# A two-layer MLP's output turned into rows by VectorE in 32x32 blocks instead of by TensorE

## The chip, the cores and the metric

The kernel runs on one core of a Trainium2 chip. The metric is the device time of one execution in microseconds. Before the change the median of three runs is 1579.02 us (1576.81 to 1579.77). Names of engines: PE is TensorE (PEld its weight loads), DVE is VectorE, ACT is ScalarE, POOL is GpSimd, SP is the engine that issues most DMAs. All arithmetic is fp32; a product that has to be exact enough is made of three single-pass products of parts (high x high, high x low, low x high).

## The reference

Attention through 32 packed queries per head, then two MLPs over 4608 tokens (8 batches of 576) of 512 channels, with 2048 hidden channels. The change touches the last MLP's output and its gate.

```python
p_packed = sm_attn(p, k, v)
out = sm_attn(q, p_packed, p_packed)                 # 8 batches, 8 heads, 576 tokens, 64
x = out.transpose(0, 2, 1, 3).reshape(B * S, H * D)  # 4608 x 512
h = x @ w_in                                         # first MLP, 512 -> 2048
g = h * (1.0 / (1.0 + np.exp(-h)))
x = g @ w_out                                        # 2048 -> 512
h = x @ w_in2                                        # second MLP
relu6 = np.clip(h + 3.0, 0.0, 6.0)
g = h * relu6 / 6.0
return (g @ w_out2).astype(np.float32)               # 4608 x 512
```

The weights arrive as 64-bit floats, and the kernel itself turns them into fp32 parts.

## The kernel before

Attention and the first MLP are woven into nine token blocks (`block`, L868): eight of 512 tokens, one for each batch, and a ninth of the 64 last tokens of all batches. A block holds its first layer's result as four accumulators in PSUM, [128 channels, 512 tokens] each. Tokens stand there in the order i, p for token 4p + i, because the queries were read that way. At the block's end the accumulators are copied to SBUF, two by ACT (L909) and two by DVE (L911), and stored to a scratch tensor `x1d` in DRAM (L912), channels first. A planner places the attention steps of the following blocks between the matmuls.

Meanwhile `Prep` (L244) prepares the second MLP's weights, 16 units for `w_in` and 16 for `w_out`, a step at a time: load (L264), two ACT operations, two on DVE, an addition on POOL that joins the two halves of each number into `c` (L293), sums on DVE (L296 to L299), the high parts on ACT, the low parts on POOL, three stores to DRAM.

The second MLP (`Second`) works on five pairs of token blocks, three of 2 x 512 tokens and two of 2 x 384. Both of its layers use a scheme of seven products for a 2 x 2 split of the weights and tokens. For each pair there are two passes:
- The hidden pass (`hidden`, L1034) has 16 chunks of seven products, six matmuls each (L1107 to L1109). Each chunk uses three PSUM banks of eight. ACT and DVE add the products up; then ACT makes relu(h + 3) (L1051) and, one product later, DVE makes min(., 6) x h (L1054).
- The projection (`project`, L1157) has seven products in four steps each, twelve matmuls a step (L1197 to L1200). An operand is split into a high part on ACT (L1145) and a low part on DVE (L1150) two steps before its use. The sums of the products are `o1`, `ou`, `ov` and `oc`, each [128 channels, 2, N tokens].

The output must be rows of tokens, but these sums have channels on the partitions. `store` (L1218) takes 128 tokens: four 128x128 transposes on TensorE against an identity into a PSUM bank (L1224), a copy on ACT that multiplies by 1/6 (L1226), a store from SP (L1230 for the eight batches, L1234 for the block of last tokens). `ou` and `ov` are stored in the last steps of their own projection (L1209), `oc` and `o1` during the next pair's hidden pass (L1114); in the last pair `oc` goes in the projection too and only `o1` is left for the end.

Weights stream into four tiles `ws` (L967 to L969); a tile is loaded again, from SP, as soon as TensorE has used it. Every engine's instructions run in the order in which this code writes them.

Of the kernel before, what the change touches and what calls it, by code (L numbers as in the profile page):

```python
# [18 lines left out]
def tile_pack_attention_two_mlps(ctx: ExitStack, tc, q, k, v, p, w_in1, w_out1, w_in2, w_out2, out):  # L19
# [8 lines left out]
    nc = tc.nc  # L28
# [41 lines left out]
    nc.vector.memset(mask, 0.0)  # L70
    for h in range(HQ):
        nc.vector.memset(mask[h * NP:(h + 1) * NP, h, :], 1.0)
    three = const.tile([P, 1], F32, name="three")
    nc.vector.memset(three, 3.0)
    d1s, d2s = {}, {}
    x1d = [dram.tile([KC, P, T], F32, name=f"x1d{j}", tag=f"x1d{j}") for j in range(NBLK)]

# [166 lines left out]
    class Prep:  # L244
# [11 lines left out]
        def load(self, u):  # L256

            kind, f, h = self.units[u]
            raw = self.pool.tile([P, 2 * T], I32, tag="praw", name="praw", bufs=2)
            for n, to in enumerate(raw.rearrange("p (n r) -> n p r", n=2)):  # L260
                src = self.src[kind](f + n * HF)
                if kind == "out":
                    src = src.rearrange("p a (r f) -> p (a r) f", r=4)
                nc.sync.dma_start(out=to.rearrange("p (r f) -> p r f", r=2), in_=src[:, h:4:2])  # L264
            raws["p", u] = raw

        def step(self):
# [6 lines left out]
        def all(self):  # L274
            self.load(0)
            for _ in range(6):
                yield
            for u, (kind, f, h) in enumerate(self.units):
                key = "p", u
                c = self.pool.tile([P, 8, P], F32, tag="c8", name="c8")  # L280
                hi = self.pool.tile([P, S7, P], F32, tag="hi7", name="hi7", bufs=2)
                conv_begin(key, self.room)
                yield
                yield
                conv_bits(key)
                yield
                if u + 1 < len(self.units):
                    self.load(u + 1)
                yield
                x, r = (t.rearrange("p (n r f) -> p n r f", n=2, r=2) for t in raws.pop(key))  # L290
                a = c[:, 0:4].bitcast(I32)
                a = a.rearrange("p (n r) f -> p n r f", n=2) if kind == "in" else a.rearrange("p (r n) f -> p n r f", n=2)
                nc.gpsimd.tensor_add(out=a, in0=x, in1=r)  # L293
                yield

                nc.vector.tensor_add(out=c[:, 4], in0=c[:, 2], in1=c[:, 3])  # L296
                nc.vector.tensor_sub(out=c[:, 6], in0=c[:, 0], in1=c[:, 2])
                nc.vector.tensor_sub(out=c[:, 5], in0=c[:, 4], in1=c[:, 0])
                nc.vector.tensor_sub(out=c[:, 7], in0=c[:, 1], in1=c[:, 5])  # L299
                yield  # L300
                nc.scalar.copy(out=hi[:, 0:2].bitcast(F32R), in_=c[:, 0:2])
                nc.scalar.copy(out=hi[:, 2:7].bitcast(F32R), in_=c[:, 3:8])
                yield
                nc.gpsimd.tensor_sub(out=c[:, 0:2].bitcast(F32R), in0=c[:, 0:2], in1=hi[:, 0:2])
                nc.gpsimd.tensor_sub(out=c[:, 3:8].bitcast(F32R), in0=c[:, 3:8], in1=hi[:, 2:7])
                yield
                yield
                to = w2[kind][f].rearrange("s p f -> p s f")
                nc.sync.dma_start(out=to[:, :, h * P:(h + 1) * P], in_=hi)
                nc.sync.dma_start(out=to[:, 0:2, (2 + h) * P:(3 + h) * P], in_=c[:, 0:2])  # L310
                nc.sync.dma_start(out=to[:, 2:7, (2 + h) * P:(3 + h) * P], in_=c[:, 3:8])
# [556 lines left out]
    def block(j, nxt, boundary):  # L868

        acc = [ps_acc.tile([P, T], F32, tag=f"acc{e}", name=f"acc{e}") for e in range(KC)]  # L870
        gs = {}
        fat = j in (0, B)
        total = ((6 if not fat else 12) + 12) * NF
        at_ = [0]

        def tick(n, calm=False):
            at_[0] += n
            plan.tick(n, at_[0] / total, calm)

        def projects(f, between=None):  # L880
            w = made["out", f] if j == 0 or f % 2 == 0 else have_out.pop((j, f))
            g = gs.pop(f)
            for e in range(KC):
                project(f, e, g, w, acc)
                tick(3)
                if e == 1 and between:
                    between()
            projected[0] = j * NF + f
        for f in range(NF):
            if not fat and f % GF == 0:  # L890
                plan.finish(lambda key: key[:3] == ("m", j, f // GF))
            g = hidden(j, f, lambda: tick(3), nxt)
            gs[f] = split_g(g)
            tick(0, True)
            nxt(f, True)
            if f == 2:
                left()
            if f >= 2:
                projects(f - 2, lambda: nxt(f, False))
            nxt(f, True)  # L900
        boundary()
        for f in (NF - 2, NF - 1):
            projects(f)
        plan.finish()
        for e2 in range(0, KC, 2):
            o = gp.tile([P, 2, T], F32, tag="x1", name="x1", bufs=2)
            for e in (e2, e2 + 1):
                if e % 2:
                    nc.scalar.copy(out=o[:, 1, :], in_=acc[e])  # L909
                else:  # L910
                    nc.vector.tensor_copy(out=o[:, 0, :], in_=acc[e])  # L911
            leave.append(lambda e2=e2, o=o: nc.sync.dma_start(out=x1d[j][e2:e2 + 2].rearrange("e p t -> p e t"), in_=o))  # L912
        if j == B:
            left()
# [23 lines left out]
    class Second:  # L938
# [95 lines left out]
        def hidden(self, n):  # L1034
# [13 lines left out]

            def act(f, part, h):
                r = self.left.tile([P, N], F32, tag="hr", name="hr", bufs=4)  # L1050
                nc.scalar.activation(out=r, in_=h, func=AF.Relu, bias=three)  # L1051

                def gate():
                    nc.vector.scalar_tensor_tensor(out=self.g[part, f // 2][:, f % 2], in0=r, scalar=6.0, in1=h, op0=ALU.min, op1=ALU.mult)  # L1054

                soon(1, gate)

# [34 lines left out]
            for i, (f, k) in enumerate(seq):  # L1092
# [18 lines left out]
                    self.load_w()  # L1111
                run_later()
                after(f, k)
                if i % S7 == 5 and self.out:  # L1114
                    self.out.pop(0)()
            while later:
                run_later()
            while self.out:
                self.out.pop(0)()


        def t1(self, fd):
# [34 lines left out]
        def project(self, n):  # L1157
            X, Y, Z = [], [], []
            N = NS[n]
            o1, ou, ov, oc = (self.left.tile([P, 2, N], F32, tag=tag, name=tag) for tag in ("o1", "ou", "ov", "oc"))  # L1160
            last_pair = n == NPAIR - 1
            early = [lambda t=t: self.store(ATS[n] + N + t * P, {0: ou, 1: ov}, t) for t in range(N // P)]
            if last_pair:
                early += [lambda t=t: self.store(ATS[n] + t * P, {0: oc}, t) for t in range(N // P)]

            def after(k):
                for i in range(2):
# [11 lines left out]
                        nc.scalar.copy(out=oc[:, i], in_=X[i])  # L1179
                    elif k == 4:  # L1180
                        nc.vector.tensor_add(out=o1[:, i], in0=o1[:, i], in1=Y[i])
                if k == 5:
                    nc.gpsimd.tensor_add(out=ov, in0=ov, in1=o1)

            for s in range(FD * S7):
                k, fd = ORDER_P[s // FD], s % FD
                w, ro = self.weights(), self.ro.pop(s)
# [18 lines left out]
                    self.split(s + RO - 1)  # L1206
                if self.prep and (s < 2 * FD or s // FD % 2 == 0):
                    next(self.prep, None)
                if s > FD * 5 and early:  # L1209
                    early.pop(0)()  # L1210
                yield
            if self.prep:
                for _ in self.prep:
                    pass
            for t in range(N // P):
                self.out.append(lambda t=t: self.store(ATS[n] + t * P, {1: o1} if last_pair else {0: oc, 1: o1}, t))

        def store(self, col, halves, t):  # L1218

            ps = self.bank()  # L1220
            lo, hi = min(halves) * 2 * P, (max(halves) + 1) * 2 * P
            for h, src in halves.items():
                for e in range(2):
                    nc.tensor.transpose(ps[:, (2 * h + e) * P:(2 * h + e + 1) * P], src[:, e, t * P:(t + 1) * P], ident)  # L1224
            o = self.left.tile([P, DM], F32, tag="st", name="st", bufs=3)
            nc.scalar.mul(out=o[:, lo:hi], in_=ps[:, lo:hi], mul=1.0 / 6.0)  # L1226
            j, c = divmod(col, T)
            if j < B:
                i = c // P
                nc.sync.dma_start(out=out[j * S:j * S + T, :].rearrange("(p i) e -> p i e", i=NI)[:, i, lo:hi], in_=o[:, lo:hi])  # L1230
            else:
                rows = out.rearrange("(b s) e -> b s e", s=S)[:, T:S, lo:hi]
                for i in range(P // TAIL):
                    nc.sync.dma_start(out=rows[c // TAIL + i], in_=o[i * TAIL:(i + 1) * TAIL, lo:hi])  # L1234

        def run(self):
            self.near = opened(ctx, "second_n", side="right", reuse_waits="tile")
# [7 lines left out]
            for n in range(NPAIR):  # L1245
# [2 lines left out]
                self.hidden(n)  # L1248
                for _ in self.projected:
                    pass  # L1250
            for fn in self.out:
                fn()


    class Feed:
# [262 lines left out]
```

## Time and profile before

| | before |
|---|---|
| median of three runs | 1579.02 us |
| the profiled execution's own time | 1579.41 us |
| its span, first to last instruction | 1577.6 us |
| PE busy, matmuls | 1531.3 us (97%) |
| DVE busy | 1018.2 us (65%) |
| ACT busy | 793.8 us (50%) |
| POOL busy | 191.1 us (12%) |
| mean granted clock of PE | 0.990 |

Busy time is the time in which an engine executes something. A matmul's own duration overlaps with the next one's, so what a matmul costs is read from the distance between starts. A releaser is the instruction that ended an engine's wait. The second MLP's first matmul starts at 862.58 us.

### The profile page before, as it was taken

The page shows a single profiled execution, that of the slowest core. Times are in us where ns is not written, and L with a number is a line of the kernel's source. Part 1 is how long each engine was busy: PE and PEld are TensorE (multiplying, and loading weights), DVE is VectorE, ACT ScalarE, POOL GpSimd, SP SyncE. Part 2 cuts the span into 40 slices and gives each one's busy share as a digit, 9 for nine tenths or more (in the row PEclk, how much of TensorE's full clock was granted, in tenths as well). Part 3 has the DMA queues.
Part 4 walks back from the last instruction along what each step waited for, and adds up shares of the span by engine and source line. Part 5 has one row for each costly group of instructions (what it writes and reads, how often), then busy time and mean ns, then how long its engine had stood idle before and what let it go on. Part 6 is the DMA issues. An engine that isn't in the chain of part 4 may idle for free.

```text
span 1577.6 us, 22053 instructions
## 1 busy us (share of the span) xinstructions
PE 1531.3 (97%) x7724; PEld 1246.2 (79%) x7724; DVE 1018.2 (65%) x1630; ACT 793.8 (50%) x1279; POOL 191.1 (12%) x171
## 2 busy tenths in 40 slices
PE   6899998999999999999999999999999999999998
PEld 3577766767777777778878888888888888999998
DVE  5876455755576465653452678767876687777775
ACT  4876545744566546654353334543454344444443
POOL 1433011111120111112232000000000000000000
PEclk9899999999999999999999999999999999999999
DMA  8899686977678776758596567666766676888886
GB/s 218 276 283 299 218 229 169 273 213 210 180 227 229 227 171 194 243 173 247 178 336 192 193 202 239 208 213 206 232 211 213 203 224 222 268 288 263 268 250 203
DMA packets 394639, 358.55 MB, mean 227 GB/s; under 512 B 155040, under 2 KB 281760, under 8 KB 394528
## 3 DMA queue, kind: packets, MB, share of 16 engines
q1 hardware_dynamic: 383152, 342.45, 72.2%
q10 hardware_dynamic: 11376, 14.68, 2.9%
q8 instruction: 62, 1.02, 0.3%
q14 instruction: 49, 0.40, 0.1%
HBM read 295.17 MB, written 61.87 MB: 226 GB/s over the span
## 4 chain that ended last, share of the span: by engine, by line
PE 86%; DMA 4%; ACT 4%; DVE 3%; issue 1%; SPq 1%; POOL 0%; DVEq 0%; POOLq 0%; ACTq 0%
PE acc L857 8%; PE b L1109 7%; PE b L1107 7%; PE b L1108 7%; PE b L1197 7%; PE acc L858 7%; PE acc L859 7%; PE b L1199 7%; PE b L1200 7%; PE hps L834 4%; PE hps L836 4%; PE hps L835 4%; PE abank L407 1%; PE abank L495 1%; PE b L1224 1%
## 5 line engine op out<-in xcount | busy, mean ns | idle before, releaser
L850 DVE TENSOR_TENSOR gl<-hps,gh 128x512 fp32r<-128x512 f32 x144 | 98.9, 687 | 170.0 <-ACT gh L849 169.6
L1199 PE MATMUL b<-ro,ws 128*128 128x512 f32 (+1 forms) x560 | 207.6, 371 | 0.0
L1107 PE MATMUL b<-xc,ws 128*128 128x512 f32 (+1 forms) x560 | 207.0, 370 | 0.0
L1200 PE MATMUL b<-ro,ws 128*128 128x512 f32 (+1 forms) x560 | 205.8, 367 | 0.0
L1109 PE MATMUL b<-xc,ws 128*128 128x512 f32 (+1 forms) x560 | 205.7, 367 | 0.0
L1108 PE MATMUL b<-xc,ws 128*128 128x512 f32 (+1 forms) x560 | 205.6, 367 | 0.0
L1150 DVE TENSOR_TENSOR ro<-g,ro 128x1024 fp32r<-128x1024 f32 (+1 forms) x140 | 161.6, 1160 | 48.4 <-ACT ro L1145 48.1
L1145 ACT CAST ro<-g 128x1024 fp32r<-128x1024 f32 (+1 forms) x140 | 133.2, 966 | 96.3 <-PE b L1197 45.4
L842 ACT ACTIVATE hps<-hps 128x512 f32<-128x512 f32 x144 | 84.0, 583 | 136.7 <-PE hps L836 133.2
L1197 PE MATMUL b<-ro,ws 128*128 128x512 f32 (+1 forms) x560 | 138.4, 368 | 0.5 <-DVE ro L1150 0.4
L857 PE MATMUL acc<-gh,wo 128*128 128x512 f32 x288 | 117.9, 409 | 0.9 <-ACT gh L849 0.9
L857 PE MATMUL acc<-gh,wr 128*128 128x512 f32 x288 | 118.2, 411 | 0.0
L1109 PEld LDWEIGHTS b<-xc,ws 128*128 128x128 f32 x560 | 105.1, 188 | 13.2
L1108 PEld LDWEIGHTS b<-xc,ws 128*128 128x128 f32 x560 | 105.2, 188 | 12.9
L1199 PEld LDWEIGHTS b<-ro,ws 128*128 128x128 f32 x560 | 105.2, 188 | 12.8
L1107 PEld LDWEIGHTS b<-xc,ws 128*128 128x128 f32 x560 | 105.1, 188 | 12.9
L1200 PEld LDWEIGHTS b<-ro,ws 128*128 128x128 f32 x560 | 105.2, 188 | 12.8
L1197 PEld LDWEIGHTS b<-ro,ws 128*128 128x128 f32 x560 | 102.4, 188 | 15.5 <-DVE ro L1150 2.4
L858 PE MATMUL acc<-gl,wo 128*128 128x512 f32 x288 | 113.6, 395 | 0.8 <-DVE gl L850 0.8
L858 PE MATMUL acc<-gl,wr 128*128 128x512 f32 x288 | 114.2, 397 | 0.0
L859 PE MATMUL acc<-gh,wr 128*128 128x512 f32 x288 | 113.9, 395 | 0.0
L859 PE MATMUL acc<-gh,wo 128*128 128x512 f32 x288 | 113.5, 394 | 0.0
(256 smaller groups left out, 2952.2 us busy)
## 6 DMA issues: line engine op xcount, KB each, us to landing
ws<-w2in SPq DMA_DIRECT2D x280, 256.0 KB, 3.2
ws<-w2out SPq DMA_DIRECT2D x280, 256.0 KB, 3.3
wi<-w1i SPq DMA_DIRECT2D x80, 512.0 KB, 5.5
wo<-w1o SPq DMA_DIRECT2D x64, 512.0 KB, 5.4
x1d<-x SPq DMA_DIRECT2D x18, 512.0 KB, 7.4
w1i<-win SPq DMA_DIRECT2D x16, 512.0 KB, 6.4
praw<-in_moe_w_in_dram SPq DMA_DIRECT2D x32, 256.0 KB, 5.6
praw<-in_moe_w_out_dram SPq DMA_DIRECT2D x32, 256.0 KB, 4.9
```

What stands on the lines that cost most here:

```text
L850: nc.vector.tensor_sub(out=gl, in0=g, in1=f32(gh))
L857: mm(acc[e], lhsT=w[:, 0, s], rhs=gh, start=first, stop=False)
L858: mm(acc[e], lhsT=w[:, 0, s], rhs=gl, start=False, stop=False)
L859: mm(acc[e], lhsT=w[:, 1, s], rhs=gh, start=False, stop=last)
L1107: mm(ps, lhsT=wh, rhs=xs[k][:, 0, c], start=first, stop=False, skip_group_check=True)
L1108: mm(ps, lhsT=wh, rhs=xs[k][:, 1, c], start=False, stop=False, skip_group_check=True)
L1109: mm(ps, lhsT=wl, rhs=xs[k][:, 0, c], start=False, stop=last, skip_group_check=True)
L1145: nc.scalar.copy(out=t[:, 0], in_=v)
L1150: nc.vector.tensor_sub(out=t[:, 1], in0=self.operand(s), in1=f32(t[:, 0]))
L1197: mm(acc[i], lhsT=wh, rhs=ro[:, 1, f], start=False, stop=last, skip_group_check=True)
L1199: mm(acc[i], lhsT=wh, rhs=ro[:, 0, f], start=first, stop=False, skip_group_check=True)
L1200: mm(acc[i], lhsT=wl, rhs=ro[:, 0, f], start=False, stop=False, skip_group_check=True)
```

## The change

The output is turned by VectorE. Its transpose works on 32x32 blocks: of a [128, N] source each block of 32 partitions and 32 columns is turned in place. So one partition group g of 32 channels gives, for each 32 tokens, 32 rows of 32 channels, on the partitions of that same group. For these to be neighbours in a row of the output, the columns of `w_out` are dealt anew when they are prepared: group g of every one of the four 128-channel parts belongs to the output columns from 128 g on. Four transposes (two for each of two sums) fill a tile `rows[t]` of [128, N/32, 128], and four stores, one for each g, each carry 32 partitions in pieces of 512 bytes.

- `Prep` loads `w_out` in runs of 64 numbers instead of 128, and POOL's addition writes runs of 32.
- The 1/6 goes into the gate: relu(h/6 + 1/2), then min(., 1) x h.
- The block-end copies write the tokens in natural order, which is a write with a step of four elements (all blocks but the ninth).
- The transposes and stores of pairs 0 to 3 all move into the next pair's hidden pass, one item at every second product. In the last pair six transposes stand in the projection, two after the last addition, and its last twelve stores go out from SP and ACT in turn.

```diff
-                    src = src.rearrange("p a (r f) -> p (a r) f", r=4)
-                nc.sync.dma_start(out=to.rearrange("p (r f) -> p r f", r=2), in_=src[:, h:4:2])
+                    src = src.rearrange("p a (b i f) -> p (a b) i f", b=4, i=2)
+                    nc.sync.dma_start(out=to.rearrange("p (b f) -> p b f", b=4), in_=src[:, :, h])
...
+                else:
+                    x, r = (t.rearrange("p (b r f) -> p b r f", b=8, r=2) for t in (x, r))
+                    a = a.rearrange("p (r n) (b f) -> p (n b) r f", n=2, b=4)
                 nc.gpsimd.tensor_add(out=a, in0=x, in1=r)
...
-                if e % 2:
-                    nc.scalar.copy(out=o[:, 1, :], in_=acc[e])
-                else:
-                    nc.vector.tensor_copy(out=o[:, 0, :], in_=acc[e])
+                to, src = o[:, e % 2, :], acc[e]
+                if j < B:
+                    to, src = to.rearrange("p (t i) -> p i t", i=NI), src.rearrange("p (i t) -> p i t", i=NI)
+                (nc.scalar.copy if e % 2 else nc.vector.tensor_copy)(out=to, in_=src)
...
-                nc.scalar.activation(out=r, in_=h, func=AF.Relu, bias=three)
+                nc.scalar.activation(out=r, in_=h, func=AF.Relu, bias=half, scale=1.0 / 6.0)
...
-                if i % S7 == 5 and self.out:
-                    self.out.pop(0)()
+                if i % 2:
+                    self.put()
...
+            rows = [self.left.tile([P, N // NP, P], F32, tag=f"st{t}", name=f"st{t}") for t in range(2)]
...
+            def turn(t, h, src):
+                for i in range(2):
+                    turns.append(lambda i=i: nc.vector.transpose(out=rows[t][:, :, (2 * i + h) * NP:(2 * i + h + 1) * NP], in_=src[:, i]))
...
+                        if last_pair:
+                            turns.pop(0)()
...
+            for t, h, src in ((1, 0, ou), (1, 1, ov), (0, 0, oc), (0, 1, o1)):
+                turn(t, h, src)
+            early, late = self.stores(ATS[n] + N, rows[1], N), self.stores(ATS[n], rows[0], N)
...
-                if s > FD * 5 and early:
-                    early.pop(0)()
+                if last_pair and s >= FD * 4 and s % FD in (1, 2):
+                    turns.pop(0)()
+                for _ in range(2 if last_pair and s > FD * 5 + 2 else 0):
+                    if early:
+                        early.pop(0)()
...
+            if not last_pair:
+                early = [fn for t in turns[0:4] for fn in (t, None)] + early
+                late = [fn for t in turns[4:8] for fn in (t, None)] + late
+            self.out += early + late
...
+        def stores(self, at_, src, m):
...
+                if j < B:
+                    pieces = [(out[j * S + c:j * S + c + w].rearrange("(m r) e -> r m e", r=NP), part)]
...
+                for to, rows in pieces:
+                    for g in range(P // NP):
+                        s = slice(g * NP, (g + 1) * NP)
+                        fns.append(lambda queue=nc.sync, to=to, rows=rows, g=g, s=s: queue.dma_start(out=to[:, :, g * P:(g + 1) * P], in_=rows[s]))
...
-            for fn in self.out:
-                fn()
+            for i, fn in enumerate(self.out):
+                fn((nc.sync, nc.scalar)[i % 2])
```

On PE, in a hidden pass before, a group of four transposes (of `oc` and `o1` against `ident`) stands between two products:

```order
L1108 MATMUL b<-xc_9153,ws 128x512
L1109 MATMUL b<-xc_9153,ws 128x512
L1224 MATMUL b<-ident,oc 128x128 x2
L1224 MATMUL b<-ident,o_8984 128x128 x2
L1107 MATMUL b<-xc_9238,ws 128x512
L1108 MATMUL b<-xc_9238,ws 128x512
```

Of these rows the two of L1224 are gone after the change, and no 128x128 matmul is left in the second MLP.

On DVE, at the start of a hidden pass after the change (`hu`, `hv` and `h` are sums of products, `g` the gate's result, `st` the row tile; line numbers are those of the changed kernel):

```order
L1190 TENSOR_TENSOR o_8984<-o_8984,b 128x512 x2
L1073 TENSOR_TENSOR hu<-h_9599,b 128x512
L1173 STREAM_TRANSPOSE st_8989<-ou 128x16x32
L1076 TENSOR_TENSOR hv<-h_9599,b 128x512
L1077 TENSOR_TENSOR hv<-hv,b 128x512
L1060 SCALAR_TENSOR_TENSOR g_9579<-hr,hv 128x512
L1173 STREAM_TRANSPOSE st_8989<-ou 128x16x32
L1060 SCALAR_TENSOR_TENSOR g_9576<-hr,b 128x512
L1073 TENSOR_TENSOR hu<-h_9643,b 128x512
```

The transposes stand between the same additions and gates, which keep their order.

On DVE, at the end of the last pair after the change (`oc` and `o` are the sums that leave last):

```order
L1156 TENSOR_TENSOR ro<-g_13269,ro 128x768
L1173 STREAM_TRANSPOSE st_13895<-oc 128x12x32 x2
L1190 TENSOR_TENSOR o_13891<-o_13891,b 128x384
L1173 STREAM_TRANSPOSE st_13895<-o_13891 128x12x32
L1190 TENSOR_TENSOR o_13891<-o_13891,b 128x384
L1173 STREAM_TRANSPOSE st_13895<-o_13891 128x12x32
```

Where before the kernel ended on DVE with the two additions, and six transposes on PE, three copies on ACT and four stores followed, a transpose now stands behind each addition, and then the twelve stores.

## Rows read from the trace of the kernel before

**Rows 1.** The page's head, its part 1 for PE, its part 2 for the clock

```profile
span 1577.6 us, 22053 instructions
PE 1531.3 (97%) x7724; PEld 1246.2 (79%) x7724; DVE 1018.2 (65%) x1630; ACT 793.8 (50%) x1279; POOL 191.1 (12%) x171
PEclk9899999999999999999999999999999999999999
```

**Rows 2.** Busy time by stretch: length, busy (instructions) of engines, clock, DMA share, GB/s

```profile
1020.00:1173.00 153.00, 152.97 (x691) 126.28 (x690) 115.53 (x133) 67.61 (x88) 2.40 (x1) 1.00 0.68 215
1173.00:1326.00 153.00, 152.97 (x690) 126.33 (x689) 112.45 (x134) 66.80 (x89) 2.40 (x1) 1.00 0.67 212
```

**Rows 3.** PE's waits from 860 us on: for whom, us, times, longest

```profile
PE b L1224 <- DVE o L1181: 0.5, 1, 0.5
PE b L1197 <- DVE ro L1150: 0.4, 1, 0.4
```

**Rows 4.** Timeline of PE around one group: start, duration, line, operation

```profile
1024.61 0.39 PE L1107 MATMUL b<-xc,ws 128*128 128x512 f32 x1
...
1025.06 0.39 PE L1109 MATMUL b<-xc,ws 128*128 128x512 f32 x1
1025.29 0.38 PE L1224 MATMUL b<-ident,oc 128*128 128x128 f32 x2
1025.51 0.38 PE L1224 MATMUL b<-ident,o 128*128 128x128 f32 x2
...
1025.96 0.39 PE L1108 MATMUL b<-xc,ws 128*128 128x512 f32 x1
```

**Rows 5.** The chain that ended last, at the same group: start, share in us

```profile
1025.45 0.44 PE b L1224 x4
```

**Rows 6.** Line 393, a block transpose on DVE: ns min/median/max

```profile
L393 DVE STREAM_TRANSPOSE T<-nat x48: 668/702/712, 175.1 to 667.7; 128x512 f32<-128x512 f32 x48
```

**Rows 7.** DVE in the first 30 us of a hidden pass

```profile
1016.00:1046.00 30.00, 17.57 (x25) 1.00 0.66 208
```

**Rows 8.** Lines 909, 911 and 174; timeline of a block's first use of a gate

```profile
L909 ACT COPY x<-acc x18: 577/587/589, 167.3 to 862.8; 128x512 f32<-128x512 f32 x18
L911 DVE COPY x<-acc x18: 652/678/692, 167.6 to 862.1; 128x512 f32<-128x512 f32 x18
L174 ACT ACTIVATE pr<-praw x32: 662/670/693, 184.3 to 840.8; 128x512 f32<-128x512 f32 x32
454.92 0.69 DVE L850 TENSOR_TENSOR gl<-hps,gh 128x512 fp32r<-128x512 f32 x1
456.87 0.39 PE L857 MATMUL acc<-gh,wr 128*128 128x512 f32 x1
```

**Rows 9.** Line 293 on POOL; DVE's wait for it from 560 to 860 us

```profile
L293 POOL TENSOR_TENSOR c<-pr x32: 1267/1289/2021, 191.3 to 844.8; 128x512 int32<-128x512 int32 x32
DVE c L296 <- POOL c L293: 14.3, 7, 5.6
```

**Rows 10.** Timeline of the end: the last two additions

```profile
1570.76 1.02 DVE L1181 TENSOR_TENSOR o<-o,b 128x384 f32<-128x384 f32 x2 [4.15 <-PE b L1197]
```

**Rows 11.** DMA issues by line (ns, starts), SP's waits, time to landing (KB, us)

```profile
L1230 SPq DMA_DIRECT2D out_dram<-st x34: 337/338/525, 1000.4 to 1573.1; - x34
L1234 SPq DMA_DIRECT2D out_dram<-st x10: 472/587/1576, 1557.4 to 1574.5; - x10
L342 SPq DMA_DIRECT2D nat<-in_k_dram x96: 579/635/1895, 102.2 to 564.3; - x96
SPq L969 <- PE b L1109: 190.6, 134, 1.8
SPq L969 <- PE b L1197: 187.0, 132, 2.2
ws<-w2out SPq DMA_DIRECT2D x280, 256.0 KB, 3.3
```

More of the change, by code (lines that the diff above doesn't have):

```diff
@@ L72, in tile_pack_attention_two_mlps @@
         nc.vector.memset(mask[h * NP:(h + 1) * NP, h, :], 1.0)
-    three = const.tile([P, 1], F32, name="three")
-    nc.vector.memset(three, 3.0)
+    half = const.tile([P, 1], F32, name="half")
+    nc.vector.memset(half, 0.5)
     d1s, d2s = {}, {}
@@ L262, in load @@
                 if kind == "out":
-                    src = src.rearrange("p a (r f) -> p (a r) f", r=4)
-                nc.sync.dma_start(out=to.rearrange("p (r f) -> p r f", r=2), in_=src[:, h:4:2])
+                    src = src.rearrange("p a (b i f) -> p (a b) i f", b=4, i=2)
+                    nc.sync.dma_start(out=to.rearrange("p (b f) -> p b f", b=4), in_=src[:, :, h])
+                else:
+                    nc.sync.dma_start(out=to.rearrange("p (r f) -> p r f", r=2), in_=src[:, h:4:2])
             raws["p", u] = raw
@@ L289, in all @@
                 yield
-                x, r = (t.rearrange("p (n r f) -> p n r f", n=2, r=2) for t in raws.pop(key))
+                x, r = raws.pop(key)
                 a = c[:, 0:4].bitcast(I32)
-                a = a.rearrange("p (n r) f -> p n r f", n=2) if kind == "in" else a.rearrange("p (r n) f -> p n r f", n=2)
+                if kind == "in":
+                    x, r, a = x, r, a.rearrange("p n f -> p (n f)")
+                else:
+                    x, r = (t.rearrange("p (b r f) -> p b r f", b=8, r=2) for t in (x, r))
+                    a = a.rearrange("p (r n) (b f) -> p (n b) r f", n=2, b=4)
                 nc.gpsimd.tensor_add(out=a, in0=x, in1=r)
@@ L1050, in act @@
                 r = self.left.tile([P, N], F32, tag="hr", name="hr", bufs=4)
[L1051 removed]
+                nc.scalar.activation(out=r, in_=h, func=AF.Relu, bias=half, scale=1.0 / 6.0)
                 def gate():
[L1054 removed]
+                    nc.vector.scalar_tensor_tensor(out=self.g[part, f // 2][:, f % 2], in0=r, scalar=1.0, in1=h, op0=ALU.min, op1=ALU.mult)
                 soon(1, gate)
@@ L1118, in hidden @@
             while self.out:
-                self.out.pop(0)()
+                self.put()
         def t1(self, fd):
@@ L1160, in project @@
             o1, ou, ov, oc = (self.left.tile([P, 2, N], F32, tag=tag, name=tag) for tag in ("o1", "ou", "ov", "oc"))
+            rows = [self.left.tile([P, N // NP, P], F32, tag=f"st{t}", name=f"st{t}") for t in range(2)]
             last_pair = n == NPAIR - 1
-            early = [lambda t=t: self.store(ATS[n] + N + t * P, {0: ou, 1: ov}, t) for t in range(N // P)]
-            if last_pair:
-                early += [lambda t=t: self.store(ATS[n] + t * P, {0: oc}, t) for t in range(N // P)]
+            turns = []
+            def turn(t, h, src):
+                for i in range(2):
+                    turns.append(lambda i=i: nc.vector.transpose(out=rows[t][:, :, (2 * i + h) * NP:(2 * i + h + 1) * NP], in_=src[:, i]))
             def after(k):
@@ L1214, in project @@
                     pass
[L1215 to L1234, printed above, removed]
+            if not last_pair:
+                early = [fn for t in turns[0:4] for fn in (t, None)] + early
+                late = [fn for t in turns[4:8] for fn in (t, None)] + late
@@ new lines, in project, with put @@
+            self.out += early + late
+        def put(self):
+            fn = self.out.pop(0) if self.out else None
+            if fn:
+                fn()
+        def stores(self, at_, src, m):
+            fns, b0 = [], 0
+            while m:
+                j, c = divmod(at_, T)
+                w = min(m, T - c)
+                part = src[:, b0:b0 + w // NP]
+                if j < B:
+                    pieces = [(out[j * S + c:j * S + c + w].rearrange("(m r) e -> r m e", r=NP), part)]
+                else:
+                    tails = out.rearrange("(b s) e -> b s e", s=S)[c // TAIL:(c + w) // TAIL]
+                    pieces = [(tails[:, T + k * NP:T + (k + 1) * NP].rearrange("b r e -> r b e"), part[:, k::TAIL // NP]) for k in range(TAIL // NP)]
+                for to, rows in pieces:
+                    for g in range(P // NP):
+                        s = slice(g * NP, (g + 1) * NP)
+                        fns.append(lambda queue=nc.sync, to=to, rows=rows, g=g, s=s: queue.dma_start(out=to[:, :, g * P:(g + 1) * P], in_=rows[s]))
+                at_, b0, m = at_ + w, b0 + w // NP, m - w
+            return fns
```

## Prediction

> **What bounds the kernel now.** I read the page's busy shares first, then the same shares by stretch, then TensorE's own waits, and only then single lines. [...] The change lies almost wholly in the second MLP, which is everything after 862 us. There the 153 us around one pair of token blocks are covered by TensorE to 152.97 us; DVE has 112 to 116 us of work in the same stretch, ACT 67 to 68, the DMA engines 67 to 68% of their time [rows 2]. The waits agree: from 860 us to the end TensorE waited 0.9 us in all, 0.5 of it for the last addition of the kernel [rows 3]. So in this half an instruction taken off TensorE's queue shortens the span by what it took there, until some other engine becomes late; and work put on DVE or on the DMA queues costs nothing until it makes TensorE wait.
>
> **What goes from TensorE.** 4608 tokens are 36 tiles of 128, with four 128x128 transposes each: 144. In the order they stand as 33 groups of four and six groups of two (last pair only); the last three groups of two come after the last matmul and belong to the end, below. What a group costs is read from the starts around one. From L1107 at 1024.61 to L1109 at 1025.06 two undisturbed steps take 0.45 us (0.225 each); from there to the second matmul behind the group, L1108 at 1025.96, two steps and four transposes take 0.90. So the four cost 0.45 us [rows 4]. The chain of waits puts 0.44 on the same group [rows 5]. I take 0.445: 33 x 0.445 = 14.7 us, plus three groups of two inside the last pair at half of it, 3 x 0.22 = 0.7. Together **15.4 us**, all on TensorE's queue between matmuls that wait for nothing, so all on the path.
>
> **What comes to DVE.** 40 block transposes: eight in each of five pairs, 24 of 128x512 and 16 of 128x384. The same operation on the same amount takes 0.70 us in the first MLP [rows 6]; at 384 columns three quarters to four fifths of it, 0.56. Sum 24 x 0.70 + 16 x 0.56 = 25.8 us. In pairs 0 to 3 they stand in the next pair's hidden pass, one to every four products (5.4 us of TensorE). DVE has 17.6 us of work in the first 30 us there [rows 7], so four more transposes make it 20.4 of 30. What is queued behind such a transpose is an addition or a gate that frees a PSUM bank; with eight banks and three per hidden chunk the first bank of chunk f is asked for again in chunk f+2, about ten products or 13 us after its last matmul, against 2 to 4 us of DVE and ACT work. A delay of 0.7 us is covered; without that cover it would be at most the 25.8 us. In the last pair six of the eight stand between the splits of products 5 to 7, and a split is made two steps before its use. I take 0. The price if the cover were partly gone is a rival below. ACT loses 39 scaled copies (some 22 us), which gives nothing, since TensorE does not wait for ACT here [rows 3].
>
> **The stores.** Each pair's output now leaves in stores that read 32 partitions and write 512-byte pieces, where a store before read 128 partitions and wrote 2 KB rows. A 2 KB-row store costs SP 0.34 us to issue; the nearest row for a quarter of the partitions cut into 512 pieces is 0.635 us [rows 11]. So 8 or 12 stores a pair add at most 3.5 us to SP in 150, and SP spends 190.6 + 187.0 us waiting for TensorE to free weight tiles [rows 11]. What is queued behind a store on SP is a weight load; there are four weight tiles, a tile is refilled three chunks before it is needed (3 x 12 matmuls x 0.225 = 8.1 us, three quarters of it, 6.1, at 384 columns) and a load lands in 3.3 us [rows 11]. Hidden: 0, with up to 1 us for the sum.
>
> **The block ends of the first MLP.** 16 copies on ACT and 16 on DVE that empty the accumulators now write with a 16-byte step. No row shows such a write. From below it costs what the dense copy does, 0.59 and 0.68 us; ACT's operation that reads with an 8-byte step takes 0.67. From above I take the slowest engine on this shape, POOL's 1.29 us [rows 8, 9]. At the block end near 450 us the gate of the new block's first chunk is split by 455.61 (454.92 + 0.69) and first used by L857 at 456.87: 1.26 us to spare [rows 8]. The upper end delays ACT by 2 x 0.70 = 1.4 us, so 0.14 us a block, 1.1 us over eight. Value 0 (nearest is the stepped read), bounds 0 and 1.1.
>
> **Weight preparation.** 16 of POOL's additions change from runs of 128 to runs of 32; bounds 1.29 us as now and 2.02, the longest seen. DVE already waits 14.3 us for that operation in 560 to 860 us [rows 9], and TensorE's list of waits names none of it. The 32 loads that feed it are cut finer, with a unit's time of lead. Value 0, upper end 1 us. The gate's new constants keep the same two instructions.
>
> **The end.** Before: the last addition starts at 1570.76, the last store is issued at 1574.5, the span ends at 1577.6, so 3.1 us after that issue [rows 10, 11]; 6.84 us in all. After: two additions (0.51 each) and two transposes (0.56) alternate on DVE, 2.2 us with hand-overs, and all twelve stores wait for the second transpose, since each carries columns of all four. They go out from SP and ACT, six each, so the last starts 5 issues later: 5 x 0.34 = 1.7 or 5 x 0.635 = 3.2 us. Plus 3.1: 7.0 to 8.5 us, **0.2 to 1.7 us longer**; I take 1.0, an issue of 0.48.
>
> The row that bears on these stores is the 64 KB load into 32 partitions, which costs more to issue than a full-width transfer four times its size [rows 11]. [...]
>
> **Sum.** Against the profiled execution: 1577.6 - 15.4 + 1.0 = 1563.2 us of span; the profiled execution's time, 1579.41, lies 1.8 above its span, which gives 1565.0. It was 0.4 above the median of 1579.02, so I predict **1564.6 us**.
>
> **Rivals.**
> *Weight loads or DVE arrive late (about 1572).* 36 stores in the hidden passes, each on a quarter of the partitions, may hold up the loads behind them, or the transposes may push DVE's split or addition past its use. If each of 36 stores or 40 transposes makes TensorE wait 0.2 us, 7 to 8 us of the gain are gone. For it: DVE is the second busiest engine, and the DMA share is 0.67 to 0.68 [rows 2]. Against it: the leads worked out above, some 4 us for a load and 9 for a bank, and 0.4 us of such waits in 700 us now [rows 3]. Chance 0.08.
>
> *The stepped copies at the block ends (slower, 1583).* Mechanism: ACT and DVE write each element 16 bytes from the one before; the copy stands ahead of the new block's first activation on ACT and of its split on DVE, and TensorE waits at the first L857 of the block. It begins to cost once a copy takes 0.59 + 1.26/2 = 1.2 us. To end at 1583 it must eat the 14.4 us and 4 more, 18.4 / 8 = 2.3 us a block, with the 1.26 spare 3.6 us for two copies: 2.4 us a copy, four times the dense one. For it: no row shows that write. Against it: the 8-byte step in the nearest row adds 0.08 to 0.59 [rows 8]. Chance 0.03.
>
> [...]
>
> *The change does not do what it says (1579).* Were transposes left on TensorE, nothing would move; the order shows none behind the second MLP's matmuls. Something close to no change would otherwise need the first rival at twice its price. Chance 0.03.
>
> **How the numbers follow.** Forecast 0.86, the rivals 0.08, 0.03 and 0.03. The forecast's own range: low, the short end (0.8 us less), the fast end of run-to-run differences (1576.81 is 2.2 below the median): 1561.6. High: the long end +0.7, block ends +1.1, preparation and loads +1.0, a slow run +0.8, and a little of the first rival: 1569. I give **1561 to 1569**. A measurement of this kernel can tell about 0.2% from no change, 3.2 us. The forecast and the first rival are faster by more: 0.94. Within 0.2%: 0.03. Slower: 0.03.
>
> **What would show it.** Right: no 128x128 matmul after 862 us; 8 x 0.445 = 3.6 us less per full pair; steps of 0.225 us through the whole hidden pass; TensorE's waits still under 2 us there; some 26 us of block transposes on DVE at 0.70 and 0.56 us; 7 to 8.5 us from the last addition's start to the end. Wrong: TensorE waits for `ws` or for a bank in the first third of a hidden pass (first rival); L857 waiting for ACT or DVE at the start of blocks with copies above 1.2 us (second); transposes far from 0.70 us, or an end over 9 us.

## The result, and the profile after

The changed kernel takes **1563.68 us** (median of 6 runs, 1561.1 to 1566.02), the kernel before 1577.96 beside it (median of 6, 1576.35 to 1579.77): ratio 0.9908, with an interval of 0.9896 to 0.9921. The forecast was 1564.6 us, in a range of 1561 to 1569.

One statement ahead of this section has to be put right, and one figure added. The hidden pass has **eight** chunks of seven products, not sixteen: 56 products, and at every second one a place for a transpose or a store, 28 places. The eight transposes of a pair, every other place, and its 8 stores fill 24 of them, with pair 3's 12 stores all 28. The figure is what the twelve stores at the end carry, 384 tokens x 512 channels x 4 bytes = **0.79 MB**: the transposes gather whole rows of the output, so no store of these tokens can leave before the last half of the channels is there. Before, half of that, 0.39 MB, had gone out earlier.

The page of the changed kernel: its head, part 1 for each engine, part 2 for the clock (compare [rows 1]).

```profile
span 1561.6 us, 21697 instructions
PE 1512.7 (97%) x7580; PEld 1230.8 (79%) x7580; DVE 1044.3 (67%) x1670; ACT 782.5 (50%) x1240; POOL 190.4 (12%) x171
PEclk9899999999999999999999999999999999999999
```

TensorE runs 7724 - 7580 = 144 instructions fewer, one for each transpose, and is busy 18.6 us less. DVE runs 40 more and is busy 26.1 us more. TensorE is still the engine that bounds the kernel. Its waits from 855 us on are one row (engine, for whom, us in all, times, longest), the same as the second of [rows 3]:

```profile
PE b L1211 <- DVE ro L1156: 0.4, 1, 0.4
```

Busy time by stretch, columns as in [rows 2], around the same pair of blocks:

```profile
1020.00:1170.00 150.00, 149.97 (x662) 123.88 (x661) 119.58 (x141) 64.22 (x81) 2.40 (x1) 1.00 0.71 221
1323.00:1449.00 126.00, 125.90 (x726) 125.50 (x725) 101.00 (x156) 54.55 (x87) 1.85 (x1) 1.00 0.89 280
1340.00:1360.00 20.00, 20.00 (x117) 19.92 (x116) 16.08 (x31) 8.03 (x16) 0.00 (x0) 1.00 0.96 307
```

TensorE is covered wholly, DVE has 120 us of 150. The second row is the first pair of 384 columns and the third the start of its hidden pass: weights are asked for faster there, the DMA engines are busy 96% of the time, and TensorE still does not wait. Both rows come back below.

The new operations, one row for each source tile of the transposes and each engine of the block-end copies, then POOL's addition and the stores (ns min/median/max, first and last start, shapes):

```profile
L1173 DVE STREAM_TRANSPOSE st<-ou x10: 568/705/708, 1016.5 to 1534.3; 128x512 f32<-128x512 f32 x6, 128x384 f32<-128x384 f32 x4
...
L1173 DVE STREAM_TRANSPOSE st<-o x10: 570/703/705, 1060.7 to 1554.0; 128x512 f32<-128x512 f32 x6, 128x384 f32<-128x384 f32 x4
...
L917 ACT COPY x<-acc x18: 585/1066/1117, 166.8 to 860.5; 128x512 f32<-128x512 f32 x18
L917 DVE COPY x<-acc x18: 691/1066/1080, 167.2 to 859.8; 128x512 f32<-128x512 f32 x18
...
L299 POOL TENSOR_TENSOR c<-pr x32: 1267/1290/1468, 190.8 to 845.5; 128x512 int32<-128x512 int32 x32
...
L1257 SPq DMA_DIRECT2D out_dram<-st x50: 315/430/1130, 1038.5 to 1559.1; - x50
...
L1257 ACTq DMA_DIRECT2D out_dram<-st x6: 378/460/1117, 1554.7 to 1558.2; - x6
```

A transpose takes 0.70 us on 512 columns and 0.57 on 384, as in [rows 6] and as scaled from it. The copies with the 16-byte step take 1.07 us against 0.59 and 0.68 dense [rows 8]. POOL's addition is unchanged [rows 9]. A store on a quarter of the partitions costs its queue 0.43 us, between the two bounds of [rows 11].

The end of the changed kernel, DVE's timeline and the issuing queues' (start, duration, engine, line; several of one kind in a row share one row; compare [rows 10]):

```profile
1552.41 0.55 DVE L1190 TENSOR_TENSOR o<-o,b 128x384 f32<-128x384 f32 x1 [1.98 <-PE b L1211]
1553.00 0.58 DVE L1173 STREAM_TRANSPOSE st<-o 128x384 f32<-128x384 f32 x1
1553.50 0.52 DVE L1190 TENSOR_TENSOR o<-o,b 128x384 f32<-128x384 f32 x1
1554.05 0.58 DVE L1173 STREAM_TRANSPOSE st<-o 128x384 f32<-128x384 f32 x1
...
1554.66 4.89 SPq L1257 DMA_DIRECT2D out_dram<-st  x6
...
1554.66 4.02 ACTq L1257 DMA_DIRECT2D out_dram<-st  x6
```

What SP waited for from 1550 us on, and the same stretch by busy time (the last two columns are the DMA share and GB/s):

```profile
SPq L1257 <- DVE st L1173: 5.1, 1, 5.1
SPq L1257 <- DMA out_dram<-st: 1.9, 2, 1.1
```
```profile
1556.00:1558.00 2.00, 0.00 (x0) 0.00 (x0) 0.00 (x0) 0.00 (x0) 0.00 (x0) 0.50 0.99 209
1558.00:1560.00 2.00, 0.00 (x0) 0.00 (x0) 0.00 (x0) 0.00 (x0) 0.00 (x0) 0.50 0.50 123
```

From the start of the last two additions to the end it is 1561.6 - 1552.41 = 9.19 us, against 1577.6 - 1570.76 = 6.84 before [rows 10]. Addition and transpose alternate as foreseen and the stores start 2.25 us after 1552.41. But then the six on SP take 4.9 us, 1.9 of it waiting until earlier stores have landed, while the DMA engines are busy 99% of the time at only 209 GB/s.

The span falls by 16.0 us in three parts. The second MLP's first matmul starts 2.29 us earlier (862.58, now 860.29); from it to the last two additions it is 692.12 us instead of 708.18, **16.06 less**; the end is **2.35 longer**. The first part can't be read as an effect: over the twelve profiles of this study that start ran from 857.0 to 864.5, with two of the changed kernel itself at 860.3 and 857.0.

### The profile page after: what moved, and what is told of

Read it like the earlier page. It is cut to its first block, busy times and chain, and to the rows that moved or that the text cites. A ratio compares the mean times of both kernels' runs of the same rounds, so it can differ in the third digit from the quotient of the medians.

```text
span 1561.6 us, 21697 instructions
## 1 busy us (share of the span) xinstructions
PE 1512.7 (97%) x7580; PEld 1230.8 (79%) x7580; DVE 1044.3 (67%) x1670; ACT 782.5 (50%) x1240; POOL 190.4 (12%) x171
## 4 chain that ended last, share of the span: by engine, by line
PE 87%; ACT 4%; DVE 3%; DMA 3%; issue 1%; SPq 1%; POOL 0%; ACTq 0%; POOLq 0%; DVEq 0%
PE acc L863 8%; PE b L1114 7%; PE b L1113 7%; PE b L1115 7%; PE b L1211 7%; PE acc L864 7%; PE acc L865 7%; PE b L1214 7%; PE b L1213 7%; PE hps L840 4%; PE hps L842 4%; PE hps L841 4%; PE abank L413 1%; PE abank L501 1%; PE abank L623 1%
```

## The experiments

Two lengths serve below: the **middle**, from the second MLP's first matmul to the start of the last two additions (708.18 us before, 692.12 changed), and the **end**, from there to the end of the span (6.84, 9.19). By a second profile of the changed kernel they repeat to 692.46 and 9.20. Ratios are to the kernel before.

### te_back: TensorE's transposes alone

All of the change stays, and 138 transposes go back on TensorE at about their old places, their results unread.

```diff
+                if i % S7 == 5 and self.back:
+                    self.back.pop(0)()
...
+        def idle_transposes(self, srcs, t):
+            ps = self.bank()
+            for h, src in enumerate(srcs):
+                for e in range(2):
+                    nc.tensor.transpose(ps[:, (2 * h + e) * P:(2 * h + e + 1) * P], src[:, e, t * P:(t + 1) * P], ident)
```

> The changed kernel with the 128x128 transposes put back on TensorE where they stood before (33 groups of four, three of two), their results read by nobody; the output still goes through VectorE. My theory (TensorE's queue time is the gain): 138 transposes at 0.11 us give the second MLP 15 to 16 us back, about 1579 us. Rival (the gain came from the freed ACT copies and PSUM banks, or from a shorter first MLP): ACT's copies stay away here, so less than 8 us comes back, below 1572 us.

Measured 1579.59 us (12 runs), ratio 1.0008 (0.9997 to 1.0019): all of the gain is gone. Middle 708.25, 16.1 more than the changed kernel; end 9.01. ACT's 39 copies stay away here, so nothing came from them. A PSUM bank for each group is taken again, but TensorE's waits from 855 us on are no longer than without it:

```profile
PE b L1217 <- DVE ro L1159: 0.4, 1, 0.4
```

So the time is the transposes on TensorE's queue and not waits for banks. 16.1 / 138 = **0.117 us** for each transpose, 0.47 for a group of four.

### dense_copies: the stepped write at the block ends

The copies write densely again, which leaves out the reordering of the tokens.

```diff
-                if j < B:
+                if False:
```

> The changed kernel with the block-end copies of the first MLP dense again; it leaves out the reordering of the tokens, so the rows of the output stand in another order. The copies should fall from 1.07 to 0.59 us on ACT and 0.68 us on DVE. My theory (the copies lie beside TensorE's work, 1.26 us to spare): no change, 1563.7 within 1.5 us, and the second MLP starts within 0.5 us of the other runs. Rival (stepped copies hold up the new block): two copies per engine and block, 8 x 0.96 = up to 7.7 us faster, 1556 us, and an earlier start of the second MLP by as much.

Line 917 of this kernel:

```profile
L917 ACT COPY x<-acc x18: 577/588/589, 166.4 to 862.5; 128x512 f32<-128x512 f32 x18
L917 DVE COPY x<-acc x18: 654/676/692, 166.7 to 861.8; 128x512 f32<-128x512 f32 x18
```

1564.21 us (6 runs), ratio 0.9914 (0.9897 to 0.993): no difference from the changed kernel, though each copy is 0.4 to 0.5 us shorter, and the second MLP starts no earlier (862.28 us). A stepped copy takes 1.07 us on either engine against 0.59 dense on ACT and 0.68 on DVE, and all of the difference is covered.

### turns_twice: DVE's cover

Every transpose of pairs 0 to 3 is made twice.

```diff
-                early = [fn for t in turns[0:4] for fn in (t, None)] + early
+                early = [fn for t in turns[0:4] for fn in (t, t)] + early
```

and the same for the other four.

> The changed kernel with each of the 32 block transposes of pairs 0 to 3 done twice: 21 us more of DVE work in the hidden passes, one transposition at every second product. My theory (the PSUM banks cover some 9 us of lag): within 1.5 us of 1563.7. Rival (DVE is nearly the limit there): 0.2 us or more per added transposition, 6 to 21 us slower, and TensorE waits for DVE in the first third of the hidden passes.

TensorE's waits in the second MLP:

```profile
PE b L1113 <- DVE hu L1073: 1.0, 2, 0.6
PE b L1113 <- DVE hv L1076: 0.7, 1, 0.7
PE b L1211 <- DVE ro L1156: 0.4, 1, 0.4
```

1565.98 us (4 runs), ratio 0.993 (0.991 to 0.9949), 2.3 us above the changed kernel where I had allowed 1.5; middle 695.27, 3.15 more. 22 us of extra work on DVE cost about 3: the cover that the prediction counted on is there, and at twice the load it begins to fail. The last row is in the changed kernel too; the other three waits, 1.7 us, all lie in the pairs of 384 columns (1353.8, 1357.9 and 1490.6 us). What the other 1.4 us are is not shown.

### stores_twice: room on the DMA queue

Every store of pairs 0 to 3 is issued a second time, into a scratch tensor.

```diff
+            if n < NPAIR - 1:
+                early = [fn for a in zip(early, self.stores(ATS[n] + N, rows[1], N, twin)) for fn in a]
+                late = [fn for a in zip(late, self.stores(ATS[n], rows[0], N, twin)) for fn in a]
...
```

> The changed kernel with each of the 36 stores of the hidden passes sent twice, the second time into a scratch tensor: twice the 32-partition, 512-byte traffic and its issues on SP. My theory (the stores lie in the weight loads' lead of 4 us): within 1.5 us of 1563.7, TensorE's waits in the second MLP still below 1 us. Rival (the stores hold up the weight loads): 0.2 us or more per added store, 7 us or more slower, and TensorE waits for ws.

1584.27 us (6 runs), ratio 1.0038 (1.0023 to 1.0053), 20.6 us above the changed kernel. My expectation that a second set hides fell. SP's timeline near 1515 us, TensorE's there, its waits, and busy time by stretch (the third column from the end is the granted clock):

```profile
1515.07 1.04 SPq L1261 DMA_DIRECT2D out_dram<-st  x1
1516.16 1.03 SPq L1261 DMA_DIRECT2D twin<-st  x1
1517.28 4.71 SPq L976 DMA_DIRECT2D ws<-w2out  x8
...
1521.44 0.66 PE L1217 MATMUL b<-ro,ws 128*128 128x384 f32 x1 [7.55 <-DMA ws<-w2out]
```
```profile
PE b L1217 <- DMA ws<-w2out: 11.9, 6, 7.5
```
```profile
1518.00:1520.00 2.00, 0.00 (x0) 0.00 (x0) 0.00 (x0) 0.00 (x0) 0.00 (x0) 0.75 1.02 200
1522.00:1524.00 2.00, 2.00 (x8) 2.00 (x7) 0.00 (x0) 0.00 (x0) 0.00 (x0) 0.50 0.97 325
1526.00:1528.00 2.00, 2.00 (x13) 2.00 (x12) 1.44 (x2) 0.53 (x1) 0.00 (x0) 1.00 0.71 199
```

The experiment mixed two things. With doubled stores a pair hands 32 or 40 items to 28 places, and the code empties the rest at once: here eight stores in a row, the last five about 1.05 us each on SP, ahead of the weight loads. TensorE waits 7.55 us, and while it stands idle its granted clock falls from 1.00 to 0.50 and is back after 1526 us. So this run can't tell the price of a burst from the price of twice the stores.

### stores_twice_spread: twice the stores without the burst

Each pair of twins takes one place.

```diff
+                early = [lambda a=a: [fn() for fn in a] for a in zip(early, self.stores(ATS[n] + N, rows[1], N, twin))]
...
```

> As stores_twice, but both copies of a store go out at the store's own place, so that none is left over for the end of a hidden pass, where eight in a row had stood ahead of the weight loads and TensorE had waited 7.5 us once. Theory (a burst ahead of the loads costs, a spread doubling does not): the stretch from the second MLP's first matmul to the last addition takes 692 to 693.5 us, as in the changed kernel (692.1), TensorE waits less than 1.5 us for ws, the median lies within 2 us of 1563.7. Rival (the bytes of the stores themselves hold up the loads): 7 us or more longer, TensorE's waits for ws spread over all pairs.

TensorE's waits in the second MLP, and busy time by stretch:

```profile
PE b L1114 <- DMA ws<-w2in: 4.6, 5, 1.8
PE b L1217 <- DMA ws<-w2out: 4.1, 4, 1.6
PE b L1114 <- DVE st L1174: 1.1, 1, 1.1
```
```profile
1016.00:1323.00 307.00, 305.26 (x1343) 251.36 (x1342) 238.69 (x286) 127.24 (x162) 4.81 (x2) 1.00 0.75 231
1323.00:1449.00 126.00, 118.02 (x660) 115.11 (x659) 93.53 (x141) 51.48 (x81) 1.86 (x1) 0.99 0.89 273
```

1580.4 us (10 runs), ratio 1.0004 (0.9991 to 1.0018), middle 707.84: all of the gain is gone again, without the drained burst, and my expectation that a spread doubling hides fell too. Nearly all waits are for weight loads. Through two pairs of 512 columns TensorE is idle 1.7 us of 307; through the first of 384 columns, 8.0 of 126. That is where the changed kernel has the DMA engines at 96% for a time (its stretch from 1340 to 1360 us, above), and where the lead of a load is 6.1 us instead of 8.1. So the first rival's mechanism is real; one set of stores lies below its threshold, two lie above it. The doubled issues on SP are not what is scarce. From 1345 to 1392 us, first what SP waits for here, then the weight loads by size and median time to landing, here and in the changed kernel:

```profile
SPq L976 <- PE b L1116: 10.0, 12, 1.7
```
```profile
ws<-w2in SPq DMA_DIRECT2D x30, 256.0 KB, 5.0
```
```profile
ws<-w2in SPq DMA_DIRECT2D x24, 256.0 KB, 4.2
```

SP still waits 10 us of 47 for TensorE to free a weight tile, but a load takes 0.8 us longer to land. The three rows of TensorE's waits above come to 9.8 of the 15.7 us. The steps are longer besides, 118.02 / 660 = 0.179 us busy for each in that stretch against 125.90 / 726 = 0.173 in the changed kernel. Part of that is the clock. TensorE is busy for only 1.1 of the 4 us from 1386 to 1390, then its granted clock falls to 0.50 and its steps take 0.32 us until about 1394:

```profile
1392.00:1394.00 2.00, 2.00 (x7) 2.00 (x7) 0.00 (x0) 0.00 (x0) 0.00 (x0) 0.50 0.95 349
```

It is at 0.50 for some 3.4 us, which by an estimate from the two step lengths loses 1.6; the rest is not split up.

### tail_swap, tail_swap_halves, tail_swap_cols: what the end is made of

The last 384 tokens leave in twelve stores because they lie in two blocks: 256 in the eighth, four stores, and 128 in the ninth, which collects the last 64 tokens of each batch entry and takes eight. The first of these kernels exchanges them with 384 tokens of pair 3 that lie in one block, so that the end has four stores with the same bytes.

```diff
+    def start(n, side):
+        return {(NPAIR - 2, 0): ATS[NPAIR - 1], (NPAIR - 1, 0): ATS[NPAIR - 2]}.get((n, side), ATS[n] + side * NS[n])
...
```

> The last two pairs exchange one token half, so that the last sums are 384 tokens of one batch: four stores at the end instead of twelve, the same 0.79 MB. From the last addition's start to the end the changed kernel takes 9.2 us. [...] Theory B (bytes at the rate of 32-partition stores, about 200 GB/s): 2.25 + 0.5 + 3.9 + 1.5 = 8.2 us. The rest of the kernel as before: 1561 to 1563 us.

1564.84 us (4 runs), ratio 0.9903 (0.9885 to 0.9922); middle 692.55, end **8.64** instead of 9.2. Eight issues fewer save 0.55 us, and the end lies 0.44 above the theory of bytes (8.2). The last term of that sum, 1.5 us, which tail_swap_cols has too, was my estimate, and no run shows it by itself; in the changed kernel's profile the DMA engines move nothing in the last 1.1 us of the span, from 1560.5 on.

The second also deals the stores to the queues by halves, so that SP sends partitions 0 to 63 while ACT sends 64 to 127; before, both began in the lower half.

```diff
-                fn((nc.sync, nc.scalar)[i % 2])
+                fn((nc.sync, nc.scalar)[i // 2 % 2])
```

> As tail_swap, with the queues dealt otherwise: SP sends partitions 0 to 63, ACT 64 to 127, so that a lower and an upper quarter are always under way together; in tail_swap two lower quarters went first, then two upper ones. Theory A (partitions decide how many DMA engines or ports work at once): 1.2 us shorter or more than tail_swap, and a higher GB/s in the last 5 us. Theory B (they don't): the same within 0.3 us.

End **7.71**, 0.93 less; theory A had asked for 1.2 or more, theory B for no more than 0.3. The last 2.5 us of transfers, of tail_swap and then of this kernel:

```profile
1559.40:1561.90 2.50, 0.00 (x0) 0.00 (x0) 0.00 (x0) 0.00 (x0) 0.00 (x0) 0.50 0.94 202
```
```profile
1562.00:1564.50 2.50, 0.00 (x0) 0.00 (x0) 0.00 (x0) 0.00 (x0) 0.00 (x0) 0.50 1.05 270
```

The same bytes move at 270 instead of 202 GB/s; how many engines or ports are at work no row shows. By the total nothing is won (1566.02 us, 4 runs, ratio 0.9912, 0.9893 to 0.9931): TensorE waits 1.9 us for weights in the last pair, and the middle is 694.52. The twelve stores now belong to pair 3's output, and with its others they exceed the 28 places, so nine go out in a row ahead of the weight loads. But they do in tail_swap too, where they take SP 4.36 us and TensorE waits for nothing; here they take 5.84. Why is not shown.

The third keeps the alternate queues and lets half of every row leave before the last addition, in pieces of 256 instead of 512 bytes, so that 0.39 MB are left for the end, as before the change.

```diff
+            if last_pair:
+                early, late = early + self.stores(start(n, 0), rows[0], N, (0, 2)), self.stores(start(n, 0), rows[0], N, (2, 4))
...
```

> As tail_swap, with the columns of w_out dealt so that each sum's 64 columns of a group lie together: the half that comes from oc can then leave before the last addition, and 0.39 MB are left for the end, in pieces of 256 bytes. Theory A (bytes decide the end): 2.25 + 0.6 + 2.0 + 1.5 = 6.3 us from the last addition's start to the end, some 2 us less than tail_swap. Theory B (the number of pieces decides, it is the same 1536): as tail_swap within 0.4 us. The finer loads of w_out in the first MLP, 256 bytes instead of 512, should stay hidden; if not, the second MLP starts later than 863 us.

1566.11 us (4 runs), ratio 0.9913 (0.9898 to 0.9928), end **6.78**, 1.86 less than tail_swap: nearer to the theory of bytes (6.3) than to that of pieces (as tail_swap, 8.64). Middle 693.27, with 0.6 us of a wait for weights.

### even_end and after_again: all three together

Exchange, halves and columns, and in the last pair's hidden pass a place at every product, so that nothing is left to be drained (pair 3's 8 transposes and 20 stores take every other one of 56 places).

```diff
-                if i % 2:
+                if i % 2 or n == NPAIR - 1:
                     self.put()
...
```

> The exchanged token half, the 64-column halves and the queues dealt by partition halves together, and the last pair's hidden pass offers a place for a store at every product instead of every second, so that the 20 stores of the pair before are spread and none is left for its end. My theory: 692.1 us from the second MLP's first matmul to the last addition, as in the changed kernel, no wait of TensorE for ws, and an end of 6.3 us (6.8 in tail_swap_cols less about half of the 0.9 that the queues gave) instead of 9.2: 2.9 us faster than the changed kernel beside it, 1560.5 to 1562 us. Rival (the stores cost the weight loads in the 384-column pair what the end gains): TensorE waits for ws there, 693.5 us or more, and no faster than the changed kernel.

> The changed kernel itself once more, on the same chip as even_end, for the comparison: 1562 to 1566 us, an end of 9.2 us, and the second MLP's first matmul between 858 and 864 us, as in the runs whose first MLP is the same.

Middle 692.13, with no wait for weights, end **6.61**, where 6.3 was expected: the burst is gone, and the end is 2.6 us shorter than the changed kernel's. Of the three steps the dealing by halves gave little here, 6.78 to 6.61 us with 0.39 MB, where it had given 0.93 with 0.79 MB. Times 1563.2 us (4 runs; ratio 0.9908, 0.9894 to 0.9921) and, for the changed kernel beside it, 1564.89 (5 runs; 0.9919, 0.9906 to 0.9933). The intervals overlap, so the 1.7 us are not shown by the total, only by the stretch, and the 1560.5 to 1562 us that I expected were missed. Part of that is the second MLP's start, 864.46 us in this kernel's profile and 857.04 in after_again's, which is below the 858 to 864 expected. It beats the kernel before; that it beats the changed one stays open.

## Why the prediction was right, step by step

- **What bounds the kernel.** Right. TensorE waits 0.4 us in the second MLP, no 128x128 matmul is left there, and putting the transposes back takes the whole gain.
- **What goes from TensorE: -15.4.** Measured -16.06 in the middle. The mechanism was right, the term 0.7 small, because the group was measured only up to the second matmul behind it, and at one place. A later step of the kernel before, ten plain steps after L1109 at 1025.06 [rows 4], starts here:

```profile
1027.80 0.39 PE L1107 MATMUL b<-xc,ws 128*128 128x512 f32 x1
```

  That is 2.74 us for ten steps and four transposes. In the changed kernel's timeline ten steps alone take 2.26:

```profile
1024.51 0.39 PE L1113 MATMUL b<-xc,ws 128*128 128x512 f32 x1
...
1026.77 0.39 PE L1114 MATMUL b<-xc,ws 128*128 128x512 f32 x1
```

  So this group costs 0.48: the first steps behind it are a little longer too (0.23 to 0.24 us, not 0.227). Among steps of 384 columns it is less. In the kernel before, one such group and ten steps:

```profile
1336.20 0.34 PE L1109 MATMUL b<-xc,ws 128*128 128x384 f32 x1
...
1338.38 0.33 PE L1107 MATMUL b<-xc,ws 128*128 128x384 f32 x1
```

  That is 2.18 us, and 0.45 without ten steps of 0.173. 20 groups stand among steps of 512 columns and 13 among steps of 384: 20 x 0.48 + 13 x 0.45 + 3 x 0.22 = 16.1, as measured here and by te_back. The prediction's 0.445 was right for the 13 and short for the 20.
- **DVE: 25.8 us, hidden.** 26.1 us, at 0.70 and 0.57 each, no wait; turns_twice shows how much room was left. One count was off: one transpose to every 5.4 us makes five or six in 30 us, not four; DVE has 21.3 us of work from 1014 to 1044, not 20.4.
- **Stores in the hidden passes: 0, up to 1.** 0. But the reason was weaker than it read. I had weighed SP's time, of which there is plenty, and a landing time of 3.3 us; what is scarce is the DMA engines' time where the columns are 384: they are 96% busy for a time, and a load lands in 4.2 us there. The mean share of the 512-column stretches [rows 2] did not show it. Twice the stores cost 16 us.
- **Block ends: 0, bounds 0 and 1.1.** 0, at 1.07 us a copy, inside the bounds and below the 1.2 from which it was to count.
- **Preparation: 0.** POOL's 1.29 us as before, no wait of TensorE.
- **The end: +1.0, from 0.2 to 1.7.** This is the term that was mis-sized: **+2.35**, 9.19 us, beyond the 9 that I had named as a sign against me. Two omissions: the end's bytes had doubled to 0.79 MB, and twelve stores do not go out back to back, since SP waits 1.9 us for earlier ones to land. I had counted issues and kept the old 3.1 us behind the last; tail_swap, tail_swap_halves and tail_swap_cols give 0.55, 0.93 and 1.86 us to issues, partitions and bytes. The three do not add up: together, in even_end, they give 2.6.
- **The sum.** 1563.2 us of span forecast, 1561.6 measured: 0.7 less from TensorE's term, 1.35 more from the end, 2.3 less from the start of the second MLP, which no step foresaw and which lies within what that start varies. The two mis-sizings partly cancel, and the start happened to be early; without it the change is worth 16.06 - 2.35 = 13.7 us, where 14.4 was forecast. So the forecast was nearer than its terms, in part by luck.

## What to carry to other kernels

Where one engine is covered to the last tenth of a microsecond, price an instruction on it by the starts ten steps later, once for each length of step around it, and check the cover of what you move at the tightest stretch of the trace, not at the mean one. At the end of a kernel nothing hides: count the bytes that become ready only with the last result, not the store instructions, and let what is ready leave earlier. If much is left for the end, let two stores that run together read different halves of the partitions: it was worth 0.93 us with 0.79 MB here, and 0.17 with 0.39 MB.

## What the runs showed of the hardware that I had not expected

- Stores that began in the same half of the partitions moved 202 GB/s with the DMA engines 94% busy; with the lower and the upper half at once it was 270, at a share of 1.05. So here the busy share did not tell what moved. In each case this is one profile.
- A 32-partition store took between 0.315 and 1.13 us of SP's time in the changed kernel, and about 1.05 each for the last five of a row of eight.
- A wait of 7.55 us cost more than itself: TensorE went on from 1521.44 to about 1526 us at a granted clock of 0.50, 8 matmuls in 2 us where 13 stand at 1.00 (steps of 0.32 instead of 0.17 us).
